# Eight-batch attention and mixer: the last 64 tokens of two batches in one chunk of 128 rows

## The chip, the cores and the metric

The kernel runs on one core of one Trainium2 chip. The metric is the device time of a launch in microseconds, median of three runs. Of one more execution there is a profile; its span goes from the first to the last instruction.

## The reference

For each of 8 batches with 8 heads, 576 tokens and head dimension 64, a linear attention ("cosformer") is followed by a mixer of tokens and channels:

```
phi(x) = [relu(x)*cos, relu(x)*sin]            # 128 features a head; cos, sin of the token's position
x   = phi(q) (phi(k)^T v) / (phi(q) sum_s phi(k) + 1e-6)     # [8, 576, 512] with heads side by side
u   = x + (relu(x^T w_tok1) w_tok2)^T          # w_tok1 [576, 256], w_tok2 [256, 576]
out = u + relu(u w_ch1) w_ch2                  # w_ch1 [512, 1536], w_ch2 [1536, 512]
```

## The kernel before

A batch's 576 tokens are four chunks of 128 rows (`ci` 0 to 3) and a tail of 64 tokens (`ci` = `R` = 4). Everything is kept for all 128 partitions, so the tail is folded: heads 0 to 3 (or channels 0 to 255) of its 64 tokens lie in partitions 0 to 63, heads 4 to 7 (channels 256 to 511) of the same tokens in partitions 64 to 127.

A batch goes through two parts:

- `Front(b)`: features of k and q (`feature`, VectorE, written as `k_side`, `q_side`), values (`values`, mostly ScalarE), `kv` (eight matmuls of 65 columns a chunk), transposed q features (`q_trans_dma` by DMA transposes, `q_trans` on TensorE for batches 0 and 1), `num` (eight matmuls of 65 columns a chunk, then reciprocal and product on VectorE into `x_sb`), token mixing `tok1` (sum over the chunks into two `b_ps`, relu into `B`) and `tok2` (`u_ps`, the sum `u_sb` on VectorE, the copy `u_bf` on ScalarE), and the transposes of u for the channel part by DMA (`u_trans_dma`: chunks 0 to 2 in one transfer, chunk 3 and the tail in a second).
- `Channel(b)`: twelve c steps (`c_main`: four matmuls of 512 columns into `c_ps`, relu by ScalarE into `h1T`; `c_tail`: four of 64 columns into `ct_ps`), then the o steps (`o_step`: twelve matmuls of 512 columns a chunk, two a step; for the tail twelve pairs of 256 columns, one of a pair writing partitions 0 to 63, the other 64 to 127), the sum `o_sb` on VectorE and the output DMA.

The order is written out by hand. While the steps of `Channel(b)` go through TensorE, the pieces of `Front(b + 1)` are put between them: `pieces` gives a slot number to each (C + n is behind c step n, O + n behind o step n), and each engine takes its instructions in that order. `first` is the plan for batch 1, which differs: its q is transposed on TensorE (slots C+9 to O+1), and batch 0's `tok2`, which has no transposes by DMA, lies in slots C+3 to C+7 of channel 0. Batch 0's own front (`first_front`) runs ahead of everything, and turns its u by matmuls (`turned_x`, `turned_b`). All loads, DMA transposes and nearly all stores are issued by SP, in program order.

Pools: PSUM has four one-bank buffers (`ps_mm`: `c_ps`, `ct_ps`, `o_ps`, `b_ps`, `u_ps`) and two of two banks (`ps_at`: `num_ps`, `kv_ps`, `qT_ps`, and `u_ps` of batch 0).

Of the kernel before, what the change touches and what calls it, by code (L numbers as in the profile page):

```python
# [16 lines left out]
def kernel(  # L17
# [15 lines left out]
    nc = tc.nc  # L33
# [31 lines left out]
    keep = ctx.enter_context(tc.tile_pool(name="keep", bufs=2))  # L65
    o_out = ctx.enter_context(tc.tile_pool(name="o_out", bufs=4))
    phi = ctx.enter_context(tc.tile_pool(name="phi", bufs=NSC))
# [20 lines left out]

    def load_tail(dst, src, b):
        return [nc.sync.dma_start(out=dst[half(g), 0:HH, R * D:(R + 1) * D],  # L90
                                  in_=src[b, g * HH:(g + 1) * HH, SM:S, :]
                                  .rearrange("h s d -> s h d"))
                for g in range(2)]

    def tiles():
        return tuple(io.tile([P, H, NSC * D], F32, name=n) for n in ("qt", "vt", "kt"))

    io_tiles = {0: tiles()}
    qt0, vt0, kt0 = io_tiles[0]
    load_main(qt0, q, 0, 0, HH)  # L100
    load_main(qt0, q, 0, HH, H, nc.scalar)
    load_tail(qt0, q, 0)
    load_main(kt0, k, 0, 0, HH)
    k_done = load_main(kt0, k, 0, HH, H)
    load_tail(kt0, k, 0)
    load_main(vt0, v, 0, 0, HH)
    load_tail(vt0, v, 0)
    load_main(vt0, v, 0, HH, H)

    stage = keep.tile([P, NSC, Dm], F32, name="u_sb").rearrange("p c m -> p (c m)")  # L110
    w_tok1n = stage[:, 0:R * D_tok].rearrange("p (r t) -> p r t", r=R)
    w_tok2n = stage[:, R * D_tok:R * D_tok + NT * S].rearrange("p (n s) -> p n s", n=NT)
# [10 lines left out]
    w_tail1 = const.tile([P, 2, D_tok], BF16, name="w_tail1")  # L123
    w_tok2 = const.tile([P, NT, S], BF16, name="w_tok2")
# [15 lines left out]
    sin_t = const.tile([P, NSC + 2], F32, name="sin_t")  # L140
    cos_t = const.tile([P, NSC + 2], F32, name="cos_t")
    for t, bias, sc in ((sin_t, bias0, scale), (cos_t, bias_hp, -scale)):
        nc.vector.memset(t, 0.0)
        nc.scalar.activation(t[:, 0:NSC], theta, AF.Sin, bias=bias, scale=sc)
        for g in range(2):
            nc.vector.tensor_copy(t[half(g), NSC + g:NSC + g + 1], t[half(g), R:NSC])

    ones = const.tile([P, 3], BF16, name="ones")
    nc.gpsimd.memset(ones, 1.0)
    for g in range(2):  # L150
        nc.gpsimd.memset(ones[half(1 - g), 1 + g:2 + g], 0.0)


    v_augs = []
    for i in range(2):
        va = const.tile([P, NSC, H, DP], BF16, name=f"v_aug{i}")
        nc.vector.memset(va[:, :, :, D:D1], 1.0)
        v_augs.append(va)


    for g in range(2):
        nc.vector.memset(w_tail1[half(1 - g), g, :], 0.0)
    for g in range(2):
        nc.gpsimd.dma_start(out=w_tail1[half(g), g, :], in_=moe_w_tok1[SM:S, :])
# [26 lines left out]
    def permute_tok2(ki):  # L191
        nc.scalar.copy(w_tok2[:, ki, 0:SM].rearrange("t (r p) -> t r p", r=R),
                       w_tok2n[:, ki, 0:SM].rearrange("t (p r) -> t r p", r=R))
        nc.scalar.copy(w_tok2[:, ki, SM:S], w_tok2n[:, ki, SM:S])


    class Front:
        def __init__(self, b, res):
            self.qt, self.vt, self.kt = io_tiles[b]
            self.va = v_augs[b % 2]  # L200
            self.res = res

            self.padded = b > 0
            self.kp, self.qp = {}, {}

            self.qpT = once.tile([P, NSC * H, P], BF16, name="qpT")
            self.kv_sb = [small.tile([P, HH, DP], BF16, name=f"kv_sb{g}") for g in range(2)]
            self.x = once.tile([P, NSC, Dm], BF16, name="x_sb")

        def feature(self, which, ci, j, heads=(0, H), on_act=False):  # L210
            dst, src = (self.kp, self.kt) if which == "k" else (self.qp, self.qt)
            if ci not in dst:
                dst[ci] = phi.tile([P, H, 2, D], BF16, name=which + "p")
            if ci < R:
                parts = [(*heads, heads[0], ci)]
            elif self.padded:
                parts = [(g * HH, (g + 1) * HH, 0, NSC + g) for g in range(2)]
            else:
                parts = [(0, HH, 0, R)]
            for lo, hi, at, col in parts:  # L220
                w = (cos_t, sin_t)[j][:, col:col + 1]
                o_ap = dst[ci][:, lo:hi, j, :]
                i_ap = src[:, at:at + hi - lo, ci * D:(ci + 1) * D]
                if on_act:
                    nc.scalar.activation(o_ap, i_ap, AF.Relu, bias=bias0, scale=w)
                else:
                    nc.vector.tensor_scalar(o_ap, i_ap, scalar1=w, scalar2=0.0,  # L227
                                            op0=ALU.mult, op1=ALU.max)

        def values(self, ci, eng, heads=(0, H)):  # L230
            lo, hi = heads if ci < R else (0, HH)
            src = self.vt[:, lo:hi, ci * D:(ci + 1) * D]
            dst = self.va[:, ci, lo:hi, 0:D]
# [5 lines left out]
        def ksum(self, ci, heads=(0, H)):  # L239

            if not hasattr(self, "ks_ps"):
                self.ks_ps = ps_mm.tile([P, H], F32, name="ks_ps", tag="mm")
                self.ks_first = True
            for h in range(*heads):
                i, col = (h, 0) if ci < R else (h % HH, 1 + h // HH)
                nc.tensor.matmul(self.ks_ps[:, h:h + 1],
                                 self.kp[ci][:, i, :, :].rearrange("p a b -> p (a b)"),
# [8 lines left out]
        def dens(self, ci):  # L256

            if ci == 0:
                self.d_ps = ps_mm.tile([P, R * H + HH], F32, name="d_ps", tag="mm")
                self.d_sb = small.tile([P, R * H + HH, 1], F32, name="d_sb")  # L260
            if ci < R:
                each = [(slice(0, P), ci * H + h, h) for h in range(H)]
            else:
                each = [(half(g), R * H + j, g * HH + j) for j in range(HH) for g in range(2)]
            for rows, i, h in each:
                nc.tensor.matmul(self.d_ps[rows, i:i + 1], self.qpT[:, i, rows],
# [6 lines left out]
        def kv(self, ci, halves=(0, 1)):  # L273
            if ci == 0 and not hasattr(self, "kv_ps"):
                self.kv_ps = {}
                if self.padded:
                    both = ps_at.tile([P, 2, 512], F32, name="kv_ps", tag="at")
                    self.kv_ps = {g: both[:, g, :] for g in range(2)}
            if ci == 0 and not self.padded:
                for g in halves:  # L280
                    self.kv_ps[g] = ps_at.tile([P, 2, 512], F32, name="kv_ps", tag="at")[:, 0, :]
            if ci < R or self.padded:
                each = [(g, j, slice(0, P), g * HH + j) for g in halves for j in range(HH)]
            else:
                each = [(g, j, half(g), j) for j in range(HH) for g in halves]
            for g, j, rows, i in each:
                nc.tensor.matmul(self.kv_ps[g][:, j * DP:j * DP + D1],  # L287
                                 self.kp[ci][rows, i, :, :].rearrange("p a b -> p (a b)"),
                                 self.va[rows, ci, i if ci < R else j, 0:D1],
                                 start=(ci == 0 and j == 0),  # L290
                                 stop=(ci == NSC - 1 and j == HH - 1),
                                 skip_group_check=True)
# [8 lines left out]
        def q_trans(self, ci, heads=(0, H), eng=nc.scalar):  # L301
            lo, hi = heads if ci < R or self.padded else (0, HH)
# [4 lines left out]
            for h in range(lo, hi):  # L307
                nc.tensor.transpose(qT_ps[:, h - lo, :],  # L308
                                    self.qp[ci][:, h, :, :].rearrange("p a b -> p (a b)"), ident)
            dst = self.qpT[:, ci * H + lo:ci * H + hi, :]  # L310
# [5 lines left out]
        def q_trans_dma(self, ci):  # L316
            nc.sync.dma_start_transpose(out=self.qpT[:, ci * H:(ci + 1) * H, :],
                                        in_=self.qp[ci].rearrange("p h a b -> p (h a b)"))

        def num(self, ci, fill=0, dens=False):  # L320
# [3 lines left out]
            n = 2 if ci < R else 1  # L324
            for h in range(H):
                g, j = divmod(h, HH) if ci < R else (h % 2, h // 2)
                kv = self.kv_sb[g][:, j, 0:D1]
                cols = slice(j * DP, j * DP + D1)
                if ci < R:
                    nc.tensor.matmul(num_ps[:, g, cols], self.qpT[:, ci * H + h, :], kv,  # L330
                                     start=True, stop=True)
                elif self.padded:
                    nc.tensor.matmul(num_ps[:, 0, cols], self.qpT[:, R * H + g * HH + j, :], kv,
                                     start=(g == 0), stop=(g == 1))
                else:
                    nc.tensor.matmul(num_ps[half(g), 0, cols], self.qpT[:, R * H + j, half(g)], kv,
                                     start=True, stop=True)
            nv = num_ps[:, 0:n, 0:HH * DP].rearrange("p g (j d) -> p g j d", d=DP)
            if dens:
                den = self.d_sb[:, ci * H:ci * H + n * HH, :].rearrange("p (g j) o -> p g j o", g=n)  # L340
            else:
                den = small.tile([P, 2, HH, 1], F32, name="den")[:, 0:n]
# [3 lines left out]
                self.x[:, ci, 0:n * DH].rearrange("p (g j d) -> p g j d", g=n, j=HH),  # L346
# [406 lines left out]
```

## Time and profile before

| what | value |
|---|---|
| runs | 274.5, 274.86, 273.28 us (median 274.5) |
| span of the profiled execution | 271.7 us |
| around the span, against the median | 2.8 us |
| TensorE (PE) busy | 262.8 us, 97% |
| VectorE (DVE) busy | 165.4 us, 61% |
| ScalarE (ACT) busy | 123.8 us, 46% |
| DMA moved | 54.46 MB, 200 GB/s |
| granted TensorE clock | 1.000 |

The profiled execution has no launch time of its own, so its time is taken as its span and the 2.8 us by which the median of the runs lies above it. Busy time of TensorE counts overlapping matmuls once, and its ends are modelled; what one matmul costs in a stream is therefore read from start to start, not from its own duration (a matmul of 512 columns lasts 379 ns, and the next starts 215 ns after it).

### The profile page before, as it was taken

How to read it: one execution, taken by the hardware profiler on the slowest of the kernel's cores; microseconds unless marked ns; L12 is line 12 of the kernel's file. 1: busy time of each engine (PE TensorE's matmuls, PEld its weight loads, DVE VectorE, ACT ScalarE, POOL GpSimd, SP SyncE). 2: the span in 40 equal slices, each digit the busy share in tenths (PEclk: the TensorE clock that was granted, in tenths of full speed). 3: DMA queues.
4: the chain of work that ended last, by engine and by line, in shares of the span. 5: the costliest groups of instructions: out<-in, count | busy, mean ns of one | idle time of the engine just before them, and what ended most of it. 6: DMA issues, size and time to landing. Idle time of an engine off the chain costs nothing.

```text
span 271.7 us, 5917 instructions
## 1 busy us (share of the span) xinstructions
PE 262.8 (97%) x2386; PEld 145.5 (54%) x2414; DVE 165.4 (61%) x421; ACT 123.8 (46%) x235; POOL 7.8 (3%) x21
## 2 busy tenths in 40 slices
PE   7989999999999999999999999999999999999994
PEld 2566466445555456455555455455555455454542
DVE  4954696759466495649666596639666586630031
ACT  4963882055616264236616264236625364315500
POOL 3400300000000000000000000000000000000000
PEclk9999999999999999999999999999999999999999
DMA  7999999959994889868696988769795453061022
GB/s 214 371 258 300 318 189 274 355 65 297 198 321 91 240 228 215 278 161 275 134 281 186 281 165 237 243 159 278 156 325 137 151 117 80 39 183 41 0 80 97
DMA packets 95483, 54.46 MB, mean 200 GB/s; under 512 B 62688, under 2 KB 90976, under 8 KB 95456
## 3 DMA queue, kind: packets, MB, share of 16 engines
q1 hardware_dynamic: 92016, 50.28, 66.7%
q0 software_dynamic: 2832, 3.21, 7.1%
q10 hardware_dynamic: 608, 0.59, 0.7%
q8 instruction: 19, 0.31, 0.5%
q14 instruction: 8, 0.07, 0.1%
HBM read 35.85 MB, written 9.44 MB: 167 GB/s over the span
## 4 chain that ended last, share of the span: by engine, by line
PE 92%; ACT 3%; DMA 2%; DVE 1%; issue 1%; POOL 0%; POOLq 0%; ACTq 0%
PE o_ps L535 29%; PE c_ps L501 29%; PE b_ps L358 5%; PE u_ps L386 4%; PE ct_ps L520 4%; PE kv_ps L287 4%; PE idle_ps L186 3%; PE o_ps L539 3%; PE num_ps L330 3%; DMA uT<-u_bf 2%; ACT qpT L312 1%; PE b_ps L362 1%; PE c_ps L511 1%; PE u_ps L390 1%; PE qT_ps L308 1%
## 5 line engine op out<-in xcount | busy, mean ns | idle before, releaser
L535 PE MATMUL o_ps<-w_ch,h1T 128*128 128x512 bf16 x367 | 94.1, 379 | 1.2
L501 PE MATMUL c_ps<-uT,w_ch 128*128 128x512 bf16 (+2 forms) x384 | 92.2, 372 | 1.0 <-DMA uT<-u_bf 0.9
L505 ACT ACTIVATE h1T<-c_ps 128x512 bf16<-128x512 f32 x93 | 55.7, 601 | 62.6 <-PE c_ps L501 62.4
L545 DVE TENSOR_TENSOR o_sb<-o_ps,u_sb 128x512 f32<-128x512 f32 (+1 forms) x40 | 25.4, 635 | 53.1 <-PE o_ps L535 49.6
L535 PEld LDWEIGHTS <-h1T 128*128 128x128 bf16 x384 | 35.1, 98 | 35.6 <-issue 1.6
L501 PEld LDWEIGHTS <-w_ch 128*128 128x128 bf16 x384 | 32.5, 97 | 29.2 <-DMA uT<-u_bf 1.4
L520 PEld LDWEIGHTS <-w_ch 128*128 128x128 bf16 x384 | 22.0, 98 | 18.4
L393 DVE TENSOR_TENSOR u_sb<-u_ps,x_sb 128x512 f32<-128x512 f32 (+1 forms) x40 | 24.7, 633 | 9.8 <-PE u_ps L386 9.5
L395 ACT CAST u_bf<-u_sb 128x512 bf16<-128x512 f32 (+1 forms) x35 | 19.4, 574 | 18.5 <-DVE u_sb L393 16.9
L520 PE MATMUL ct_ps<-uT,w_ch 128*128 128x64 bf16 x384 | 24.1, 193 | 0.0
L368 ACT ACTIVATE B<-b_ps 128x512 bf16<-128x512 f32 x8 | 4.8, 597 | 42.1 <-PE b_ps L358 42.1
L345 DVE TENSOR_TENSOR x_sb<-num_ps,den 128x512 bf16<-128x512 f32 (+1 forms) x35 | 22.3, 638 | 1.2
L227 DVE TENSOR_SCALAR qp<-qt,cos_t 128x512 bf16<-128x512 f32 (+1 forms) x50 | 20.4, 419 | 0.9 <-DMA qt<-in_q_dram 0.9
L227 DVE TENSOR_SCALAR qp<-qt,sin_t 128x512 bf16<-128x512 f32 (+1 forms) x50 | 20.4, 419 | 0.0
L227 DVE TENSOR_SCALAR kp<-kt,cos_t 128x512 bf16<-128x512 f32 (+1 forms) x47 | 20.0, 442 | 0.3 <-DMA kt<-in_k_dram 0.3
L235 ACT CAST v_aug<-vt 128x512 bf16<-128x512 f32 (+1 forms) x34 | 18.1, 556 | 0.0
L358 PE MATMUL b_ps<-x_sb,w_tok 128*128 128x512 bf16 x63 | 17.7, 379 | 0.1
L386 PE MATMUL u_ps<-B,w_tok 128*128 128x512 bf16 x57 | 17.6, 379 | 0.1
L227 DVE TENSOR_SCALAR kp<-kt,sin_t 128x512 bf16<-128x512 f32 (+1 forms) x42 | 17.5, 430 | 0.0
L343 DVE TENSOR_SCALAR den<-num_ps 128x8 f32<-128x8 f32 (+1 forms) x35 | 5.7, 164 | 18.3 <-PE num_ps L330 17.7
L287 PE MATMUL kv_ps<-v_aug,kp 128*128 128x65 bf16 (+1 forms) x320 | 15.5, 193 | 0.3 <-ACT qpT L312 0.3
L330 PE MATMUL num_ps<-kv_sb,qpT 128*128 128x65 bf16 x256 | 14.0, 193 | 0.7 <-DVE x_sb L345 0.5
(80 smaller groups left out, 186.3 us busy)
## 6 DMA issues: line engine op xcount, KB each, us to landing
out_dram<-o_sb SPq DMA_DIRECT2D x32, 256.0 KB, 3.7
kt<-in_k_dram SPq DMA_DIRECT2D x7, 1024.0 KB, 5.9
qt<-in_q_dram SPq DMA_DIRECT2D x7, 1024.0 KB, 7.9
vt<-in_v_dram SPq DMA_DIRECT2D x7, 1024.0 KB, 6.5
w_ch<-in_moe_w_ch_dram POOLq DMA_DIRECT2D x4, 384.0 KB, 9.8
w_ch<-in_moe_w_ch_dram POOLq DMA_DIRECT2D x3, 512.0 KB, 8.8
qt<-in_q_dram SPq DMA_DIRECT2D x16, 64.0 KB, 6.2
kt<-in_k_dram SPq DMA_DIRECT2D x2, 512.0 KB, 6.5
```

The lines of the kernel that those rows point to most:

```text
L227: nc.vector.tensor_scalar(o_ap, i_ap, scalar1=w, scalar2=0.0, op0=ALU.mult, op1=ALU.max)
L287: nc.tensor.matmul(self.kv_ps[g][:, j * DP:j * DP + D1], self.kp[ci][rows, i, :, :].rearrange("p a b -> p (a b)"), self.va[rows, ci, i if ...
L330: nc.tensor.matmul(num_ps[:, g, cols], self.qpT[:, ci * H + h, :], kv, start=True, stop=True)
L345: nc.vector.tensor_mul(self.x[:, ci, 0:n * DH].rearrange("p (g j d) -> p g j d", g=n, j=HH), nv[:, :, :, 0:D], den.to_broadcast([P, n, HH, ...
L358: nc.tensor.matmul(self.b1_ps[mi], w_tok1[:, ci, cols], self.x[:, ci, :], start=(ci == 0), stop=(ci == R - 1))
L386: nc.tensor.matmul(u_ps, w_tok2[:, ki, ci * P:(ci + 1) * P], self.B1[:, ki, :], start=(ki == 0), stop=(ki == NT - 1))
L393: nc.vector.tensor_add(res["u"][:, ci, 0:n], u_ps[:, 0:n], self.x[:, ci, 0:n])
L501: nc.tensor.matmul(c_ps[:, lo:hi], w_ch1[:, ki, mi * P:(mi + 1) * P], uT[:, lo // P:hi // P, ki, :], start=(ki == 0), stop=(ki == NCC - 1))
L505: nc.scalar.activation(self.h1T[:, mi, 0:SM], c_ps, AF.Relu)
L520: nc.tensor.matmul(self.ct_ps[:, mi % 6, :], w_ch1[:, ki, mi * P:(mi + 1) * P], self.res["uT"][:, R * NCC + ki % 2, half(ki // 2)], start= ...
L535: nc.tensor.matmul(o_ps, self.h1T[:, ki, ci * P:(ci + 1) * P], w_ch2[:, ki, :], start=start, stop=stop)
L545: nc.vector.tensor_add(o_sb[:, 0:n], o_ps[:, 0:n], res["u"][:, ci, 0:n])
```

## The change

The tails of two batches (2p and 2p + 1) are put together in one chunk of 128 rows: the even batch's 64 tokens in partitions 0 to 63, the odd batch's in 64 to 127, all eight heads (512 channels) in the free dimension. A class `Tail` holds what a pair shares.

- Features of k and q of the tail are made once a pair, in the even batch's front (two instructions of 128x512 for k, two for q, instead of four and four of 128x256 for each batch); batches 0 and 1 still make their own, on 64 partitions. The DMA transpose of the q features is issued once a pair. The loads of both batches' tails come with the even batch's loads.
- `values`, `num`'s product, `tok2`'s sum and copy of the tail work on the batch's own 64 partitions, with 512 elements instead of 256. The other half of `v_aug` and of the new `x_tail` is set to zero once, so that `kv` and `tok1` can use all 128 rows.
- `tok1` and `tok2` of the tail are one matmul of 512 columns where there were two of 256; `tok2` now makes 128 rows, of which a batch uses its 64.
- The transposes of u of the tail, and its c and o, are made once a pair, in the odd batch's channel part: `c_tail` is four matmuls of 128 columns for each of 12 blocks, `o_step(R)` twelve of 512 columns. Channels of even batches have 12 c and 24 o steps and no tail, channels of odd batches 12 and 30.
- Batch 0's tail is no longer turned by matmuls ahead of its channel; its u is copied by ScalarE (`ub_tail`) behind `tok2` in slot C+7.
- The plan of an odd batch's front (3, 5, 7) has `kv` of chunk 3 and of the tail, `kv_out`, `num`, the mixing and the transposes of u one slot earlier.
- In the last channel the tail's o comes first, and chunk 3 is made last, in two halves of 256 columns.

The core of the diff:

```diff
+    class Tail:
+
+        def __init__(self, pair):
+            self.qt, self.vt, self.kt = io_tails[pair]
+            self.kp = twos.tile([P, H, 2, D], BF16, name="kp_tail")
+            self.qp = once.tile([P, H, 2, D], BF16, name="qp_tail")
+            self.qpT = twos.tile([P, H, P], BF16, name="qpT_tail")
+
+        def new_u(self):
+            self.u = twos.tile([P, Dm], F32, name="u_tail")
+            self.ub = once.tile([P, Dm], BF16, name="ub_tail")
+            self.uT = once.tile([P, NCC, P], BF16, name="uT_tail")
...
+                t = self.tail
+                dst, src = (t.kp, t.kt) if which == "k" else (t.qp, t.qt)
+                rows = self.rows if self.alone else slice(0, P)
+                w, o_ap, i_ap = w[rows], dst[rows, lo:hi, j, :], src[rows, lo:hi, :]
...
-                if ci < R:
-                    nc.tensor.matmul(self.b1_ps[mi], w_tok1[:, ci, cols], self.x[:, ci, :],
-                                     start=(ci == 0), stop=(ci == R - 1))
-                else:
-                    for g in range(2):
-                        nc.tensor.matmul(self.b1_ps[mi][:, g * DH:(g + 1) * DH],
-                                         w_tail1[:, g, cols], self.x[:, R, 0:DH],
-                                         start=False, stop=False, skip_group_check=True)
+                w = w_tok1[:, ci, cols] if ci < R else w_tail1[:, cols]
+                nc.tensor.matmul(self.b1_ps[mi], w, self.x_of(ci),
+                                 start=(ci == ORDER[0]), stop=(ci == ORDER[-1]))
...
-                for g in range(2):
-                    nc.tensor.matmul(u_ps[half(g), 0:DH], w_tok2[:, ki, SM:S],
-                                     self.B1[:, ki, g * DH:(g + 1) * DH],
-                                     start=(ki == 0), stop=(ki == NT - 1))
...
+                nc.tensor.matmul(u_ps, w_tok2[:, ki, ci * P:(ci + 1) * P],
+                                 self.B1[:, ki, :], start=(ki == 0), stop=(ki == NT - 1))
+            u = res["u"][:, ci, :] if ci < R else tail.u[rows]
+            nc.vector.tensor_add(u, u_ps[rows], self.x_of(ci)[rows])
+            if ci == R:
+                nc.scalar.copy(tail.ub[rows], u)
+            elif turn:
+                nc.scalar.copy(self.ub[:, ci, :], u)
...
+        def tail_trans_dma(self):
+            nc.sync.dma_start_transpose(out=self.tail.uT, in_=self.tail.ub)
...
+                plan += [(C + at, KV, ci) for ci, at in
+                         enumerate((2, 3, 4, 5, 6) if odd else (2, 3, 4, 6, 7))]
+                plan.append((C + (7 if odd else 8), self.kv_out))
             if first:
                 at, mix, t = (O + 4, O + 6, O + 7, O + 9, O + 10), O + 11, O + 14
+            elif odd:
+                at, mix, t = (C + 8, C + 9, C + 10, C + 11, O + 2), O + 3, O + 7
             else:
                 at, mix, t = (C + 9, C + 10, C + 11, O + 1, O + 3), O + 4, O + 8
...
-            plan += [(t + 2, self.u_trans_dma, 0, 3), (t + 3, self.u_trans_dma, 3, NSC)]
+            plan += [(t + 2, self.u_trans_dma, 0, 3), (t + 3, self.u_trans_dma, 3, R)]
+            if odd:
+                plan.append((t + 3, self.tail_trans_dma))
...
-                nc.tensor.matmul(self.ct_ps[:, mi % 6, :], w_ch1[:, ki, mi * P:(mi + 1) * P],
-                                 self.res["uT"][:, R * NCC + ki % 2, half(ki // 2)],
+                nc.tensor.matmul(self.ct_ps[:, mi % R, :], w_ch1[:, ki, mi * P:(mi + 1) * P],
+                                 self.tail.uT[:, ki, :], start=(mi % R == 0 and ki == 0),
...
-                for g in range(2):
-                    nc.tensor.matmul(o_ps[half(g), 0:DH], self.h1T[:, ki, SM:S],
-                                     w_ch2[:, ki, g * DH:(g + 1) * DH], start=start, stop=stop)
...
+                h = self.h1T[:, ki, ci * P:(ci + 1) * P] if ci < R else self.h1T_tail[:, ki, :]
+                nc.tensor.matmul(o_ps, h, w_ch2[:, ki, cols], start=ki == 0, stop=ki == NCH - 1)
...
-                rest = (2, R, 3)
-            else:
-                rest = range(NSC) if self.b == B - 1 else (0, 1, R, 2, 3)
+                rest = (2, 3)
+            elif self.b == B - 1:
+                rest = (R, 0, 1, 2)
+            else:
+                rest = (0, 1, R, 2, 3) if self.b % 2 else range(R)
             for ci in rest:
                 o_range(ci, 0, NCH)
+            if self.b == B - 1:
+
+                for g in range(2):
+                    steps.append(lambda g=g: self.o_step(R - 1, 0, NCH,
+                                                         slice(g * DH, (g + 1) * DH)))
```

More of the change, by code (lines that the diff above doesn't have):

```diff
@@ L204, in __init__, with k_of @@
             self.kp, self.qp = {}, {}
-            self.qpT = once.tile([P, NSC * H, P], BF16, name="qpT")
-            self.kv_sb = [small.tile([P, HH, DP], BF16, name=f"kv_sb{g}") for g in range(2)]
-            self.x = once.tile([P, NSC, Dm], BF16, name="x_sb")
+            self.qpT = once.tile([P, R * H, P], BF16, name="qpT")
+            self.kv_sb = [twos.tile([P, HH, DP], BF16, name=f"kv_sb{g}") for g in range(2)]
+            self.x = once.tile([P, R, Dm], BF16, name="x_sb")
+        def k_of(self, ci):
+            return self.kp[ci] if ci < R else self.tail.kp
@@ L210, in feature, with q_of, qT_of, x_of @@
+        def q_of(self, ci):
+            return self.qp[ci] if ci < R else self.tail.qp
+        def qT_of(self, ci, h):
+            return self.qpT[:, ci * H + h, :] if ci < R else self.tail.qpT[:, h, :]
+        def x_of(self, ci):
+            return self.x[:, ci, :] if ci < R else self.xt
+        def rows_of(self, ci):
+            return slice(0, P) if ci < R else self.rows
         def feature(self, which, ci, j, heads=(0, H), on_act=False):
-            dst, src = (self.kp, self.kt) if which == "k" else (self.qp, self.qt)
@@ L275, in kv @@
                 self.kv_ps = {}
-                if self.padded:
+                if halves == (0, 1):
                     both = ps_at.tile([P, 2, 512], F32, name="kv_ps", tag="at")
                     self.kv_ps = {g: both[:, g, :] for g in range(2)}
-            if ci == 0 and not self.padded:
+            if ci == 0 and halves != (0, 1):
                 for g in halves:
                     self.kv_ps[g] = ps_at.tile([P, 2, 512], F32, name="kv_ps", tag="at")[:, 0, :]
[L282 to L292, printed above, removed]
+            for g in halves:
+                for j in range(HH):
+                    nc.tensor.matmul(self.kv_ps[g][:, j * DP:j * DP + D1],
+                                     self.k_of(ci)[:, g * HH + j, :, :]
+                                     .rearrange("p a b -> p (a b)"),
+                                     self.va[:, ci, g * HH + j, 0:D1],
+                                     start=(ci == 0 and j == 0),
+                                     stop=(ci == NSC - 1 and j == HH - 1),
+                                     skip_group_check=True)
         def kv_out(self, halves=(0, 1), eng=None):
@@ L372, in tok2 @@
         def tok2(self, ci, pool=None, turn=True):
-            res = self.res
+            res, tail = self.res, self.tail
             if ci == 0:
-                res["u"] = keep.tile([P, NSC, Dm], F32, name="u_sb")
+                res["u"] = keep.tile([P, R, Dm], F32, name="u_sb")
                 if turn:
                     self.new_uT()
-                    self.ub = once.tile([P, NSC, Dm], BF16, name="u_bf")
+                    self.ub = once.tile([P, R, Dm], BF16, name="u_bf")
+            if ci == R and not hasattr(tail, "u"):
+                tail.new_u()
             if pool is None:
@@ L382, in tok2 @@
                 u_ps = pool.tile([P, Dm], F32, name="u_ps", tag="at")
-            n = Dm if ci < R else DH
+            rows = self.rows_of(ci)
             for ki in range(NT):
-                if ci < R:
-                    nc.tensor.matmul(u_ps, w_tok2[:, ki, ci * P:(ci + 1) * P],
-                                     self.B1[:, ki, :], start=(ki == 0), stop=(ki == NT - 1))
-                    continue
-                for g in range(2):
-                    nc.tensor.matmul(u_ps[half(g), 0:DH], w_tok2[:, ki, SM:S],
-                                     self.B1[:, ki, g * DH:(g + 1) * DH],
-                                     start=(ki == 0), stop=(ki == NT - 1))
@@ new lines, in tok2, with turned_x @@
+            u = res["u"][:, ci, :] if ci < R else tail.u[rows]
[4 more added lines that the diff above has]
+                nc.scalar.copy(self.ub[:, ci, :], u)
+        def new_uT(self):
+            self.res["uT"] = keep.tile([P, R * NCC, P], BF16, name="uT")
+        def turned_x(self, dst, kb, first):
+            for ci in range(R):
+                nc.tensor.matmul(dst[:, ci * P:(ci + 1) * P],
+                                 self.x[:, ci, kb * P:(kb + 1) * P], ident, start=first,
+                                 stop=False, skip_group_check=True)
@@ L549, in o_step @@
                 return
             for g in range(2):
-                eng = nc.scalar if b == B - 1 and g == 1 else nc.sync
-                eng.dma_start(out=out[b, SM:S, g * DH:(g + 1) * DH], in_=o_sb[half(g), 0:DH])
+                nc.sync.dma_start(out=out[b - 1 + g, SM:S, cols], in_=o_sb[half(g)])
         def steps(self, done):
```

288 lines of the change are left out of this document (132 added, 156 removed).

## The prediction

> **What bounds the kernel.** First the page's busy shares and the chain that ended last:
>
> ```profile
> PE 262.8 (97%) x2386; PEld 145.5 (54%) x2414; DVE 165.4 (61%) x421; ACT 123.8 (46%) x235; POOL 7.8 (3%) x21
> ...
> PE 92%; ACT 3%; DMA 2%; DVE 1%; issue 1%; POOL 0%; POOLq 0%; ACTq 0%
> ```
>
> TensorE is the bound; nearly all else waits for it. So the change is worth what it takes from TensorE's stream, less what others then make TensorE wait. The chain in order of time tells what a matmul costs in the stream:
>
> ```profile
> 57.07 4.69 DMA uT<-u_bf
> 61.81 2.79 PE c_ps L501 x24
> ...
> 92.50 2.59 PE c_ps L501 x12
> ...
> 116.28 1.31 PE o_ps L539 x24
> ...
> 122.88 2.59 PE c_ps L501 x12
> ...
> 247.10 0.86 PE c_ps L501 x4
> 248.09 0.86 PE c_ps L501 x4
> ```
>
> A channel lasts 122.88 - 92.50 = 30.38 us, all of it streaming. 512 columns cost 2.59/12 = 0.2155 us. At 61.81, 12 matmuls have 384 columns and 12 have 128; start to start in the trace these cost 0.1625 and 0.0557, each with weights of its own (2.62; the rest of 2.79 is the last one's drain). A tail's c in channel 7 takes 248.09 - 247.10 - 0.86 = 0.12 for four, 0.0293 each start to start. A pair of tail-o matmuls takes 1.31/12 = 0.109: its halves run side by side. So cost goes by columns, and folding the tail already made its columns few. TensorE's timeline shows what surrounds such half matmuls:
>
> ```profile
> 115.35 0.59 PE L386 MATMUL u_ps<-B,w_tok 128*128 128x512 bf16 x2
> 115.87 0.41 PE L390 MATMUL u_ps<-B,w_tok 128*64 128x256 bf16 x4
> 116.11 1.48 PE L539 MATMUL o_ps<-w_ch,h1T 128*64 128x256 bf16 x24
> 117.52 0.82 PE L535 MATMUL o_ps<-w_ch,h1T 128*128 128x512 bf16 x3
> ```
>
> The two matmuls at 115.35 are through at 115.78; the next full one starts at 117.52. The stretch, 1.74, is 14 pairs (1.53) and two changes of width, 0.1 each.
>
> **Steady channels.** c of the tail: 96 x 0.0293 = 2.81 a pair of batches before, 48 x 0.0557 = 2.67 after. `tok2` and o of the tail: 2 x 1.74 = 3.48 before; 2 x 0.431 + 12 x 0.2155 = 3.45 after. `kv`, `num` and `tok1` keep their columns. So the pair saves only 0.17: an even channel loses 1.41 + 1.74 - 0.43 = 2.72, an odd one gains 1.26 + 1.28 = 2.54.
>
> Waits. `num(0)` follows `kv_out` by one c step. Before: relu starts 0.2 behind c, takes 0.5, the two kv copies end 0.68 later (timeline at 102.2 to 103.4), so `num` ends 1.52 behind that c, 0.18 late. In an even channel the c step now lacks 0.24 of tail: 0.41 late. In an odd one tail columns double: not late. Per pair +0.05. The q transposes: VectorE drops the tail features (1.05 for k, 1.05 for q ahead of the last), so q of chunk 0 lands 7.3 us into the channel (96.45 + 3.16 - 92.33) as now, against 9.0 needed; chunk 3 about 12, against 14. Covered by over 1.5 us. The transposes of u in an even channel: second one issued 3.1 behind `tok2(2)`, landing 5.65 (2.55 as at 118.66), with 6.9 until the next channel; covered by 1.25. The tail's own transposes are queued behind on SP, ahead of stores and the next k load, which have a channel's time. On ScalarE and VectorE the tail's `values`, product, sums and copies go from 256 to 512 elements (0.42 to 0.69 us on VectorE), while half the features go: hidden at 61% and 46% busy; uncovered they would cost 0.27 each. Batches 2 to 5: 2 x (-0.17 + 0.05) = -0.24. Batches 6 and 7: -2.72 + 0.23 + 1.26 + (2.59 - 1.41) = -0.05.
>
> **Head.** Batch 0's tail is no longer turned: 12 matmuls of 64 columns, -0.35. Its wider features, copies and products, on 64 partitions, are priced by the 128x512 rows (no row is on 64 partitions; between the 256 and the 512 price, I take the upper): +0.1 where k's arrival and the wait for x3 do not cover them. The zero fills fall ahead of q's landing at 5.8.
>
> **Channel 0 decides.** It gives its tail c (1.41) and tail o (1.4) to channel 1, which gets 2.54 more. Does channel 0 become shorter by that?
>
> ```profile
> 36.25 0.41 DVE L393 TENSOR_TENSOR u_sb<-u_ps,x_sb 128x256 f32<-128x256 f32 x1
> 37.33 1.01 ACT L312 COPY qpT<-qT_ps 128x1024 bf16<-128x1024 bf16 x1
> 40.52 1.95 ACT L312 COPY qpT<-qT_ps 128x1024 bf16<-128x1024 bf16 x2
> 42.52 0.89 PE L287 MATMUL kv_ps<-v_aug,kp 128*128 128x65 bf16 x24 [0.31 <-ACT qpT L312]
> ```
>
> `kv` at 42.52 waits for ScalarE's last copy, and ScalarE is full from 36.8 on. The new `ub_tail` copy (C+7) stands in ScalarE's queue ahead of h1T(8) and all four copies, and waits for the tail's sum on VectorE, which has the k features and q(0) in front of it. VectorE's rows, moved by the head and with the two 0.4 us tail features, end that sum at 35.94; then copy 0.53, four relus of 0.5, four copies of 0.92: 42.15. `kv` comes 0.3 earlier, where TensorE alone would come 2.3 earlier (bounds 0 and -2.3; the ScalarE order is the nearer row). Then the tail's product takes 0.69 instead of 0.42, and `b_ps` L362 at 50.17 had only 0.06 to spare behind it: 0.3 is lost again. `tok2(2)` ends at 55.5 as before.
>
> From there TensorE needed 5.2 to the channel's end, and waited until 6.3 for the transposes at 57.07 (the 4.69 above). After, it needs 0.43 x 3 + 6 x 0.431 = 3.88. Issued at +1.57, the transposes land at +4.8 if they take 3.23 as in channel 2 (116.48 to 119.71), at +6.3 if 4.69. The DMA view of 57 to 62 us, in slices of 0.125, shows why they took longer:
>
> ```profile
> DMA  0000000000769999000000000019999999989999
> ...
> q8 instruction: 1, 0.02, 1.7%
> ```
>
> They stop from 59.0 to 60.3, after a 16 KB instruction packet began at 58.32. The page has 19 of these for 4830 TensorE instructions, one in 254. By the order of the instructions that place now falls some 70 ahead of `tok2(2)`, so I take 3.23: channel 1 starts 1.45 earlier. Its first tail c needs the tail's u transposed: issued third on SP at +5.1, landing +7.65, needed at +7.45: +0.2.
>
> **End.** Before, tail last, 3.75 from the last matmul to the end. After, half of chunk 3, 128 KB in one store: between 2.19 (64 KB) and 2.48 (256 KB) to landing, +0.15, and +0.03 for halves. For an instruction packet among the transposes of channel 6, +0.15.
>
> **The sum**, against the profiled execution (span 271.7 + 2.8 = 274.5, the median): -1.45 to the start of channel 1, + 2.54 - 0.18 + 0.2 in it, -0.24 - 0.05 for the other pairs, +0.18 and +0.15 at the end: +1.1, or 275.6. A measurement of this kernel can tell about 0.5%, 1.4 us, from no change.
>
> **Rivals.**
> 1. *The transposes wait in channel 0 stays* (4.69, or `kv` no earlier). The idle that the moved tail leaves is then wholly filled by the wait at 61.81: +2.6, 277.1. For: it is there now. Against: the interrupting packet moves. 0.28.
> 2. *Even channels end in a wait.* Cover of 1.25 is less than one interruption (1.4), and loads with two tails each are larger; at 0.9 in each of three channels, 278.3. It decides once the second transposes take over 3.8; they now take 2.55. 0.12.
> 3. *Faster.* ScalarE's order does not bind and the wait at 61.81 goes: `kv` 2.3 earlier and no loss at L362 put the start of channel 1 3.75 earlier: -3.75 + 2.56 - 0.29 + 0.33 = -1.15; without the 0.95 of waiting for the transposes that is left, -2.1, 272.4. For: ScalarE had 1.2 us idle between 34 and 36.8. Against: nearly all waits must vanish. 0.08.
> 4. *Weights not hidden.* A 98 ns weight load (page, L520's rows) showing behind each 0.0557 matmul would cost 192 x 0.042 = 8, 282.6. Against it stand the 12 at 61.81. 0.02.
> 5. That the change leaves the work where it was: TensorE's order after has 4102 instructions for 4830, so no.
>
> A rule that speaks against the change bears on rival 4: by the Trainium skill, page "TensorE: Matmul & The Clock Gate", section "Back-to-back issue gap", pairs of weight load and matmul are spaced about 81 ns at 128 columns. By that the tail's c would take 5 us more than I count, an estimate. The trace disagrees: 0.0557.
>
> **Chances.** My sum 0.50, its own range 274.4 to 276.9: within 0.5% 0.37, slower 0.12, faster 0.01. With rivals 1 and 2 slower, 3 mostly faster, 4 slower: faster 0.07, same 0.41, slower 0.52. The likeliest single case is the sum. 273.8 to 278.0 leaves out rival 4, most of 3, half of 2.
>
> **What would show it.** Right: `ct_ps` and tail `o_ps` together within 0.3 us a pair of the old; ScalarE idle behind the tail's sum near C+7, `kv` of batch 1 at about 42; even channels near 27.9 us, odd near 32.7; channel 1's c at about 60.4. Wrong: matmuls of 128 columns spaced by over 60 ns; waits for `uT` ahead of channels 3, 5, 7; `kv` of batch 1 near 40.

## The result, and the profile after

The changed kernel takes 275.64 us (median of 6, 275.25 to 276.44) where the kernel before, run beside it, takes 274.15 (273.28 to 274.86): a ratio of 1.0065, 95% interval [1.0046, 1.0084]. A second series gave 275.35 to 273.76, 1.0059 [1.0037, 1.0080]. So the change costs 1.5 to 1.6 us. Medians below are of up to 12 executions; where some of these had a granted clock of 0.991 to 0.994, these mostly lie 1.5 to 3.7 us above the others, which widens the intervals.

The profiled execution took 275.3 us. Its page gives the span, then for each engine the busy time, its share of the span and the number of instructions, then the shares of the chain that ended last.

```profile
span 273.5 us, 5131 instructions
PE 263.8 (96%) x2050; PEld 139.3 (51%) x2050; DVE 163.8 (60%) x374; ACT 128.8 (47%) x232; POOL 9.6 (4%) x22
PE 85%; DVE 6%; ACT 3%; DMA 3%; issue 1%; POOL 0%; POOLq 0%; ACTq 0%
```

There are 336 matmuls fewer (2050 for 2386), and TensorE is busy for 1.0 us more: the work was regrouped, not removed. TensorE's part of the chain fell from 92% to 85%: more of the end now hangs on VectorE, ScalarE and DMA. Where, the chain in order of time shows (start, length, what). First channel 0:

```profile
35.16 0.60 DVE u_tail L412
35.78 0.62 ACT ub_tail L414
36.40 0.97 ACT h1T L528 x2
...
40.15 1.81 ACT qpT L347 x2
42.01 0.89 PE kv_ps L321 x24
...
56.98 3.31 DMA uT<-u_bf
60.34 2.79 PE c_ps L524 x24
```

The new copy `ub_tail` waits for the tail's sum on VectorE, and everything from there to `kv` at 42.01 is ScalarE. The transposes of u now take 3.31 instead of 4.69. TensorE's timeline shows two more places (start, length, instructions; in brackets the idle time before and what ended it):

```profile
104.02 0.42 PE L362 MATMUL num_ps<-kv_sb,qpT 128*128 128x65 bf16 x8 [0.22 <-DMA qpT<-qp]
268.14 1.47 PE L557 MATMUL o_ps<-w_ch,h1T 128*128 128x256 bf16 x12 [0.52 <-DVE o_sb L562]
```

In channel 2 a q transpose landed late; the chain has it as

```profile
99.03 4.94 DMA qpT<-qp
```

At 268.14 the second half of the last chunk waits until VectorE has read the first half, since both halves lie in one PSUM tile.

The starts of the channels (first `c_ps` matmul in the timeline) and their lengths; the last column reaches to the start of the last matmul:

| | ch. 1 starts | ch. 1 | ch. 2 | ch. 3 | ch. 4 | ch. 5 | ch. 6 | ch. 7 |
|---|---|---|---|---|---|---|---|---|
| before | 61.81 | 30.52 | 30.38 | 30.38 | 30.38 | 30.38 | 30.38 | 23.44 |
| after | 60.34 | 32.79 | 28.31 | 32.75 | 27.91 | 32.75 | 27.91 | 26.59 |
| difference | -1.47 | +2.27 | -2.07 | +2.37 | -2.47 | +2.37 | -2.47 | +3.15 |

Channels 1 to 6 together change by 0.00. What channel 0 gains (1.47) is less than what channel 7 loses (3.15); with +0.14 behind the last matmul (3.89 for 3.75) that is +1.8 in the span.

### The profile page after: what moved, and what is told of

The parts are those of the page before. It is cut to its first block, busy times and chain, and to the rows that moved or that the text cites. A ratio compares the mean times of both kernels' runs of the same rounds, so it can differ in the third digit from the quotient of the medians.

```text
span 273.5 us, 5131 instructions
## 1 busy us (share of the span) xinstructions
PE 263.8 (96%) x2050; PEld 139.3 (51%) x2050; DVE 163.8 (60%) x374; ACT 128.8 (47%) x232; POOL 9.6 (4%) x22
## 4 chain that ended last, share of the span: by engine, by line
PE 85%; DVE 6%; ACT 3%; DMA 3%; issue 1%; POOL 0%; POOLq 0%; ACTq 0%
PE o_ps L557 31%; PE c_ps L524 24%; PE b_ps L385 6%; PE u_ps L409 6%; PE ct_ps L544 4%; PE idle_ps L205 4%; PE num_ps L362 3%; PE kv_ps L321 3%; DMA qpT<-qp 2%; DVE kp L264 1%; ACT qpT L347 1%; DMA uT<-u_bf 1%; ACT h1T L528 1%; DVE x_sb L372 1%; PE c_ps L534 1%
## 5 line engine op out<-in xcount | busy, mean ns | idle before, releaser
L557 PE MATMUL o_ps<-w_ch,h1T 128*128 128x512 bf16 (+1 forms) x396 | 95.1, 372 | 0.5 <-DVE o_sb L562 0.5
L524 PEld LDWEIGHTS <-w_ch 128*128 128x128 bf16 x384 | 33.1, 97 | 30.1 <-DMA uT<-u_bf 1.4
L412 DVE TENSOR_TENSOR u_sb<-u_ps,x_sb 128x512 f32<-128x512 f32 x32 | 22.1, 689 | 9.7 <-PE u_ps L409 9.6
L416 ACT CAST u_bf<-u_sb 128x512 bf16<-128x512 f32 x28 | 17.3, 618 | 17.6 <-DVE u_sb L412 17.6
L409 PE MATMUL u_ps<-B,w_tok 128*128 128x512 bf16 x80 | 22.8, 379 | 0.1
L372 DVE TENSOR_TENSOR x_sb<-num_ps,den 128x512 bf16<-128x512 f32 x28 | 19.4, 691 | 1.0
L544 PEld LDWEIGHTS <-w_ch 128*128 128x128 bf16 x192 | 14.0, 98 | 9.2
L385 PE MATMUL b_ps<-x_sb,w_tok 128*128 128x512 bf16 x64 | 17.9, 379 | 0.0
L544 PE MATMUL ct_ps<-uT_tail,w_ch 128*128 128x128 bf16 x192 | 17.2, 219 | 0.0
L264 DVE TENSOR_SCALAR qp<-qt,sin_t 128x512 bf16<-128x512 f32 (+1 forms) x35 | 15.8, 451 | 0.0
L362 PEld LDWEIGHTS <-qpT 128*128 128x128 bf16 x256 | 11.6, 98 | 7.6 <-issue 2.1
L264 DVE TENSOR_SCALAR kp<-kt,cos_t 128x512 bf16<-128x512 f32 x32 | 15.2, 479 | 0.4 <-DMA kt<-in_k_dram 0.4
```

Of the source, the lines that this page charges most:

```text
L362: nc.tensor.matmul(num_ps[:, g, j * DP:j * DP + D1], self.qT_of(ci, h), self.kv_sb[g][:, j, 0:D1], start=True, stop=True)
L372: nc.vector.tensor_mul(self.x_of(ci)[rows].rearrange("p (g j d) -> p g j d", g=2, j=HH), nv[:, :, :, 0:D], den.to_broadcast([rows.stop - r ...
L385: nc.tensor.matmul(self.b1_ps[mi], w, self.x_of(ci), start=(ci == ORDER[0]), stop=(ci == ORDER[-1]))
L409: nc.tensor.matmul(u_ps, w_tok2[:, ki, ci * P:(ci + 1) * P], self.B1[:, ki, :], start=(ki == 0), stop=(ki == NT - 1))
L412: nc.vector.tensor_add(u, u_ps[rows], self.x_of(ci)[rows])
L416: nc.scalar.copy(self.ub[:, ci, :], u)
```

## Experiments

The theory: TensorE's cost goes by columns, so sharing tails moves work and saves 0.1 to 0.2 us a pair; the loss is waits, in channel 0 (the emptied time is not used), in even channels (`num(0)` behind `kv_out`), and at the end (one PSUM tile). Rivals: narrow matmuls dearer than their columns; the features or the transposes of q bind.

**The changed kernel again**, beside the second group of variants.

> The changed kernel itself once more, on the same chip as the variants beside it, for their comparison. Expected 1.0 to 2.2 us over the kernel before.

275.35 to 273.76, +1.59; channel 1 starts at 59.88, the rest is as above except channel 2 (28.11). So channel 0's end and channel 2 differ between executions by some 0.5, the other channels by 0.01.

**The tail's c and o left out, after and before.** In both kernels `c_tail` is not called and `o_step(R)` puts out u:

```diff
-                    for m in range(tails[0], upto):
-                        self.c_tail(m)
...
+            if ci == R:
+                if hi == NCH:
+                    nc.vector.tensor_copy(o_sb, self.tail.u)
+                    ...
+                return
```

> The changed kernel with the tail's c and o matmuls left out (the tail's output is u alone; its front part stays). Theory (48 c matmuls at 0.0557 and 12 o matmuls at 0.2155 are 5.26 us a pair, and nothing hides): odd channels 27.5 to 27.7, even ones 27.9 as they are, the launch about 21.0 us shorter, 254.4. Rival (128-column matmuls show their weight loads): 26 us or more shorter.

> The kernel before with the tail's c and o matmuls left out in the same way. Theory (1.41 for c and 1.31 to 1.4 for o a batch): channels 1 to 6 of 27.6 to 27.9 instead of 30.38, the last one 2.7 shorter, channel 0 shorter by 0 to 2.8; the launch 19 to 22 us shorter, 252 to 255, so that both kernels without tails lie within 2 us of each other, the difference being channel 0's. Rival (folded tails cost more than their columns, so that pairing saves several us on TensorE): 25 us or more shorter.

After: 257.92, 17.4 less than the 275.35 with tails. Before: 256.10, 17.5 less than the 273.59 beside it. Both missed the expected saving (21.0; 19 to 22), because waits came up where the tails had been. In the first, channel 2 now stops for 1.82:

```profile
99.91 0.42 PE L362 MATMUL num_ps<-kv_sb,qpT 128*128 128x65 bf16 x8 [1.82 <-DMA qpT<-qp]
```

This transpose of q was issued at 93.07 and landed at 99.86, 1.5 behind the last store issued ahead of it (98.36). The odd channels of the first last 28.5 to 28.6, not 27.5: two of three end in a wait for the transposes of u (0.57 and 0.45), and in all three, as in channels 2 to 6 of the second, `num(0)` comes late behind `kv_out`, as in the changed kernel's even channels (0.41, see the run with `kv_out` earlier). Channel 3 of the second:

```profile
127.78 0.56 PE L330 MATMUL num_ps<-kv_sb,qpT 128*128 128x65 bf16 x8
128.18 1.03 PE L501 MATMUL c_ps<-uT,w_ch 128*128 128x512 bf16 x4
129.04 0.41 PE L330 MATMUL num_ps<-kv_sb,qpT 128*128 128x65 bf16 x8
129.28 1.03 PE L501 MATMUL c_ps<-uT,w_ch 128*128 128x512 bf16 x4
```

The late one takes 0.40 until the next c, the one after it 0.24.

So that the two kernels without tails lie 1.8 apart, about as far as with them, says little: other waits make up this distance. Channel 7, which has no front beside it, gives the clean figure: in the first it is 26.59 - 21.31 = 5.28 shorter, and 48 matmuls of 0.0557 and 12 of 0.2155 make 5.26. So the rival of dear narrow matmuls falls. Its row says the same:

```profile
74.62 0.67 PE ct_ps L544 x12
```

Two channels together last 2 x 30.38 = 60.76 before and 32.75 + 27.91 = 60.66 after: a pair saves 0.10, its waits included.

**The copy `ub_tail` later.** Batch 0's copy goes from C+7 behind o step 3:

```diff
-            if ci == R:
+            if ci == R and turn:
                 nc.scalar.copy(tail.ub[rows], u)
...
+            slots.setdefault(NCH + 3, []).append((f.tail_copy, ()))
```

> The changed kernel, with batch 0's copy of the tail's sum on ScalarE (ub_tail, slot C+7 of channel 0) moved behind o step 3. Theory (ScalarE's order holds kv in channel 0: the copy waits 2.14 us for VectorE's sum and the four qpT copies stand behind it): kv at about 40.5 instead of 42.0, channel 1 starts at about 58.9 instead of 60.3, the launch 1.5 us shorter. Rival (the transposes of q or VectorE bind, the copy's place is irrelevant): kv at 41.7 or later and no more than 0.3 us in the time.

274.80 (12), 1.0044 [1.0015, 1.0074] against before. Its chain:

```profile
33.23 1.41 DVE kp_tail L264 x2
...
35.60 0.64 PE qT_ps L343 x8
36.26 1.01 ACT qpT L347
...
41.05 0.89 PE kv_ps L321 x24
```

ScalarE takes up `qpT` at 36.26 instead of 37.38, and `kv` comes at 41.05 instead of 42.01 (41.48 in the second profile of the changed kernel): 0.4 to 1.0 earlier, not 1.5. Channel 1 starts at 59.41. The copy's place does count, so the rival's 0.3 is passed, but only two thirds or less of the expected is there: the next to bind is the tail's k features on VectorE at 33.23, which the q features and so the first `qT_ps` wait for. These two took 0.68 and 0.81 there, beside DMA issues of GpSimd, and 0.48 each in the second profile of the changed kernel; without these 0.53, `kv` would come at 40.5, as expected (an estimate). But the profile that the 42.0 comes from had lost 0.41 in the same way. In the time the gain can't be told from none.

**The first plan one slot earlier as well.**

```diff
-                at, mix, t = (O + 4, O + 6, O + 7, O + 9, O + 10), O + 11, O + 14
+                at, mix, t = (O + 3, O + 5, O + 6, O + 8, O + 9), O + 10, O + 13
```

> The changed kernel with batch 0's copy of the tail's sum behind o step 3 (as in the run that moved this copy alone: channel 1 at 59.41, with 0.90 us of waiting for the first transposes of u) and the first plan's num, mixing, tok2 and transposes of u one slot earlier. Theory (the wait ahead of channel 1 is the transposes' latency less the o work behind tok2, so one o step of 0.43 more behind it shortens the wait by that): channel 1 at about 59.0, the wait 0.5, the launch 0.4 us shorter than with the copy alone and about 1.7 shorter than the changed kernel. Rival (num then waits for kv_out, and b_ps for x_tail, for as long): channel 1 at 59.3 or later.

275.13, 1.0062 [1.0035, 1.0089]. The profile has channel 1 at 59.08, as expected, but the wait shrank by 0.05 (0.85 for 0.90), not by 0.43: against the run before, the transposes were issued 0.71 earlier and took 3.71 instead of 3.34. No gain in the time.

**Two PSUM tiles for the last chunk's halves.**

```diff
-            if lo == 0 and cols.start == 0:
+            if lo == 0:
```

> The changed kernel, with the two halves of the last chunk's o in the last channel in PSUM tiles of their own. Theory (the second half waits 0.52 us because the sum on VectorE still reads the tile that it writes): the gap at 268.1 goes, the launch 0.5 to 0.65 us shorter. Rival (the wait is only for VectorE as the engine that hands out buffers, or the store at the end takes its place): 0 to 0.2 us.

274.63, 1.0017 [0.9992, 1.0041]. The gap is gone; o runs without a stop:

```profile
264.79 4.73 PE L557 MATMUL o_ps<-w_ch,h1T 128*128 128x512 bf16 x33
```

Channel 7 lasts 25.91 instead of 26.59: 0.68. The theory holds.

**`kv_out` one slot earlier in odd batches' fronts.**

```diff
-                         enumerate((2, 3, 4, 5, 6) if odd else (2, 3, 4, 6, 7))]
-                plan.append((C + (7 if odd else 8), self.kv_out))
+                         enumerate((2, 3, 4, 5, 5) if odd else (2, 3, 4, 6, 7))]
+                plan.append((C + (6 if odd else 8), self.kv_out))
```

> The changed kernel; in the plan of odd batches' fronts kv of the tail is put into the slot of chunk 3's (C+5) and kv_out one slot earlier (C+6), so that two c steps lie ahead of num(0). Theory (num(0) in even channels waits about 0.4 us for the copies of kv): three even channels 0.3 to 0.4 us shorter each, the launch 0.7 to 1.2 us shorter. Rival (kv now waits for the features or values instead, or num's wait is for the transposed q): -0.2 to +0.6 us.

274.51, 1.0006 [0.9981, 1.0031]. Channels 4 and 6 last 27.50 instead of 27.91, 0.41 less each, the upper end of what was expected; channel 2, whose q transpose came late again (4.70), 28.10. In the changed kernel `num(0)` starts 0.26 behind the eight c matmuls ahead of it (8 x 0.2155) and takes 0.39 until the next c; with the edit it follows twelve without a gap and takes 0.25:

```profile
161.44 1.89 PE L524 MATMUL c_ps<-uT,w_ch 128*128 128x512 bf16 x8
163.43 0.56 PE L362 MATMUL num_ps<-kv_sb,qpT 128*128 128x65 bf16 x8
163.82 1.03 PE L524 MATMUL c_ps<-uT,w_ch 128*128 128x512 bf16 x4
```

```profile
162.26 2.76 PE L524 MATMUL c_ps<-uT,w_ch 128*128 128x512 bf16 x12
164.85 0.41 PE L362 MATMUL num_ps<-kv_sb,qpT 128*128 128x65 bf16 x8
165.10 1.03 PE L524 MATMUL c_ps<-uT,w_ch 128*128 128x512 bf16 x4
```

The theory holds.

**Features for each batch again.** `self.alone = True`, the odd fronts' KS, QS and q transposes of the tail back in the plan, and the unused half of the tail's features filled with zeros by GpSimd. Then the same with that fill behind batch 2's q load.

> The changed kernel, with the tail's features of k and q and their transpose made for each batch again instead of once a pair (on the batch's own 64 partitions; 12 more feature products of about 0.4 us on VectorE and three more transposes). Theory (the features lie beside TensorE's stream, so that saving them paid nothing): the time of the changed kernel within 0.3 us, the odd fronts' num without a new wait. Rival (VectorE's order holds the odd fronts, their saving is what lets kv and num lie one slot earlier): num(0) or num(1) waits in channels 2, 4 and 6, 0.3 us or more each, +0.9 us or more.

> The changed kernel with the tail's features and q transposes made for each batch again, as in the run before it (channels 2 to 7 as long as in the changed kernel, but channel 1 at 61.7), with the zero fill that this needs on GpSimd put behind batch 2's q load, so that it no longer lies at 34.7 to 35.9. Theory (what was lost there was VectorE's k_tail and q products, 1.50 and 1.16 instead of 0.48 us each, beside GpSimd's fill and DMA issues; the features themselves cost nothing): channel 1 at 59.9 to 60.4, the time within 0.4 us of the changed kernel. Rival (the extra features or transposes cost 0.8 us by themselves): channel 1 or the later channels later, 0.6 to 0.9 us over the changed kernel.

The first: 276.12, 1.0080 [1.0059, 1.0102], 0.8 above the changed kernel, against the theory. But it isn't the rival's place either: channels 4 and 6 last 27.91 as ever, channel 2 lasts 28.34, and it is channel 1 that starts late, at 61.71. Its timeline:

```profile
33.47 1.50 DVE L264 TENSOR_SCALAR kp_tail<-ktt,sin_t 64x512 bf16<-64x512 f32 x1
34.98 1.16 DVE L264 TENSOR_SCALAR qp<-qt,cos_t 128x512 bf16<-128x512 f32 x1
36.07 0.47 DVE L264 TENSOR_SCALAR qp<-qt,sin_t 128x512 bf16<-128x512 f32 x1
32.48 2.24 POOL L194 DMA_DIRECT2D w_ch<-in_moe_w_ch_dram  x3 [18.52 <-DMA qt<-in_q_dram]
34.69 1.17 POOL L722 MEMSET kp_tail<- 64x1024 bf16 x1
```

Two VectorE products took three and two and a half times their usual 0.47 beside GpSimd's issues and fill. With the fill moved away, the timeline has

```profile
33.52 0.47 DVE L264 TENSOR_SCALAR kp_tail<-ktt,sin_t 64x512 bf16<-64x512 f32 x1
34.00 0.52 DVE L264 TENSOR_SCALAR qp<-qt,cos_t 128x512 bf16<-128x512 f32 x1
```

channel 1 at 60.55, and 275.34, the changed kernel's time (ratio to before 1.0070 [1.0039, 1.0101]). So the saved features pay nothing that can be told, and the first variant's loss went with the fill. How much of the 1.50 was due to GpSimd's issues, which lie beside most of that product in this profile, stays open.

**The repairs together**: all four, and the three without the earlier first plan.

> The changed kernel with all four repairs: the copy of batch 0's tail sum later, the first plan one slot earlier, kv_out in odd fronts one slot earlier, two PSUM tiles for the last chunk's halves. Theory (the four waits are of different places and add up: 1.3 and 0.4 in channel 0, three times 0.41, 0.65 at the end): 3.4 to 3.8 us shorter than the changed kernel, about 1.5 to 2 us (0.6 to 0.7%) shorter than the kernel before; even channels 27.5, last channel 25.9. Rival (a wait that goes is replaced by the next one): less than 2 us shorter than the changed kernel.

> The changed kernel with three of the repairs: the copy of batch 0's tail sum later, kv_out in odd fronts one slot earlier, two PSUM tiles for the last chunk's halves; the first plan as it was. Theory (moving the first plan earlier brought nothing, since its transposes then met the tail loads of batch 2; the other three add up, 1.0, 0.7 to 1.2 and 0.65): 2.4 to 2.9 us shorter than the changed kernel, 0.2 to 0.5% faster than the kernel before. Rival (the earlier first plan was worth its 0.4): 273.5 or more, no faster than the kernel before.

All four: 273.33, 0.9982 [0.9956, 1.0009]; three: 273.54, 1.0005 [0.9979, 1.0032]. These are 2.0 and 1.8 less than the changed kernel, where 3.4 to 3.8 and 2.4 to 2.9 were expected; neither can be told from the kernel before. Even channels of 27.50 and the last of 25.91 are there; what is missing is channel 0 (59.64 and 60.75) and channel 2 (28.03, 28.14). In the profile of the three, channel 1 is 1.64 longer as well, at a lower clock of TensorE (last section). What holds channel 0 is seen when the variants stand side by side (us; times of landing as the trace has them for each transfer):

| | k of batch 1 landed | `kv` | transposes of u issued | last store ahead landed | transposes landed |
|---|---|---|---|---|---|
| after | 28.30 | 42.01 | 56.98 | 58.01 | 60.29 |
| after, again | 28.56 | 41.48 | 56.44 | 58.32 | 59.83 |
| two tiles | 28.34 | 42.42 | 57.39 | 59.40 | 60.89 |
| `kv_out` earlier | 29.86 | 43.15 | 58.12 | 60.68 | 62.19 |
| features each | 28.80 | 43.39 | 58.36 | 58.38 | 61.66 |
| the same, late fill | 28.62 | 41.77 | 56.74 | 59.00 | 60.51 |
| copy later | 28.23 | 41.05 | 56.03 | 57.87 | 59.36 |
| and first plan earlier | 28.07 | 40.76 | 55.32 | 57.46 | 59.03 |
| all four | 27.86 | 40.69 | 55.24 | 58.01 | 59.59 |
| three | 28.52 | 40.87 | 55.84 | 59.19 | 60.70 |

In each row the transposes land at the later of two times, within 0.1: 3.3 behind their issue, or 1.5 behind the landing of the last store of `o_sb` issued ahead of them. Issued more than 1.8 ahead of that landing, they gain nothing unless the store lands earlier, and it was issued behind batch 2's loads, which now carry the tails of two batches (two DMAs of 128 KB to a load, where there were two of 64 KB): the last of them landed at 54.80 and this store at 56.10 before, 56.72 and 58.01 after. That fits all ten rows, and the changed kernel without tails (issued at 57.15, landed at 60.45). In the kernel before and in the run that follows, where the store landed 1.0 and 1.2 ahead of the issue and an instruction packet fell among the transposes, it doesn't apply. No run moved those loads, so the cause is argued, not shown.

**The kernel before, moved in the instruction stream.**

```diff
-        busy(idle_ps, 12)
+        busy(idle_ps, 9)
+        busy(idle_ps[:, 0:16], 24)
```

> The kernel before, with its idle warm-up at the start made of 9 matmuls of 512 columns and 24 of 16 columns instead of 12 of 512, so that every later TensorE instruction moves by 21 matmuls in the stream and the work stays the same. Theory (a 16 KB instruction packet on a DMA queue holds up the transposes of u in channel 0, and its place goes by the count of instructions): the packet falls elsewhere, the transposes take about 3.2 instead of 4.69 us, the wait ahead of channel 1 (0.94) is gone, and channel 1 starts about 0.95 earlier; other channels may lose some of it where the packet now falls among their transposes. Rival (the first transposes are slow by themselves or by the loads around them): they still take 4.4 to 4.8 us and the time stays within 0.3 us.

272.74, 0.9954 [0.9929, 0.9978]: 1.2 us gained by changing no work. Channel 1 starts at 60.75, with this timeline and chain:

```profile
60.75 0.99 PE L501 MATMUL c_ps<-uT,w_ch 128*128 128x384 bf16 x5 [0.20 <-DMA uT<-u_bf]
```

```profile
56.75 3.96 DMA uT<-u_bf
```

The wait fell from 0.94 to 0.20, as the transposes took 0.73 less. The other 0.32 of the 1.06 by which channel 1 starts earlier lies ahead of them (`kv` at 42.19 for 42.52), and its cause is open. The packet did not leave the transposes' time: the trace has it at 57.59, 0.84 behind their issue (58.32 and 1.25 before), where it costs 0.7 instead of 1.4, against the 3.3 of the changed kernel's transposes. So the place of the packet counts, but the expectation that it would miss the transposes, and take the whole wait with it, was wrong.

## Why the prediction was right, and where it was wrong

The forecast of 275.6 against 275.64, slower with a chance of 0.52, was right. The parts:

- **Columns.** Right. `ct_ps` takes 0.67 for 12 matmuls (0.0557 each), a pair saves 0.10 (0.17 less 0.05 predicted), and this row, with the 5.28 of channel 7, excludes rival 4. (Its time would have been 283.6, with its 8 on top of the sum; nothing rests on that.)
- **`num(0)`** late by 0.41 in even channels, not in odd ones: right, and taking it away gives 0.41.
- **Channel 0.** Right: `kv` at 42.01 (42.15 predicted), transposes of 3.31 (3.23), channel 1 at 60.34 (60.4). Its reason, ScalarE's order, holds in part: with the copy moved, 0.4 to 1.0 comes back.
- **Tail transposes in channel 1**, +0.2: too much. Channel 1 is 0.04 longer than channels 3 and 5.
- **Covered by over 1.5 us** (the q transposes) failed in channel 2: 0.40 in the first profile, 0.20 in the second. An 8 KB and a 16 KB instruction packet (at 99.67 and 100.31) fell among them, and one took 4.94, where others take 2.79. By these rows it is rival 2's mechanism at another transfer, which the prediction had weighed only for the transposes of u; no run moved these packets, and with the copy moved both fell there too (4.48) and channel 2 lost nothing.
- **Batches 6 and 7**, -0.05: measured -2.47 + 3.15 = +0.68. The term that failed is "+0.03 for halves": making chunk 3 in two halves was priced as matmuls, and the wait of the second half for VectorE's read of the tile both share was overlooked. The run with two tiles gives 0.68.
- **End**: +0.15 predicted, +0.14.
- **Sum.** The span grew by 1.8, not by 1.1: +0.7 in channels 6 and 7 and +0.4 in channel 2 beyond the forecast, -0.3 in channel 1, and -0.2 since the packet expected among channel 6's transposes (0.15) cost nothing there (27.91, as channel 4) and the halves are counted above. That the number came out all the same is partly luck: the 2.8 us put around the span was 1.0 too much. The executions listed with their spans have 1.8 around it (275.3 and 273.5), so the profiled execution of before was one of about 273.5 and not of the median.

## What to carry to other kernels

Folding two half-empty tiles into a full one saves next to nothing where an instruction already costs what its columns cost; compare column counts before and after, not instruction counts. When work is moved off a stage, find what that stage waits for next (here a copy in ScalarE's queue, then VectorE's features, then, it seems, a transpose behind a store), and expect only the distance to it. Work split into halves needs two output buffers, or the second half waits for the first one's reader.

## What the runs showed of the hardware

- **VectorE beside GpSimd.** A product of 0.47 us took up to 1.50 while GpSimd issued DMAs or filled zeros. In the ten profiles of the changed kernel and its variants without that fill beside them, the products beside GpSimd's issues at 32 to 36 lost 0.04 to 0.76 in all. By the Trainium skill, page "SBUF — State Buffer", section "SBUF: two separate sides", the two engines share a port pair as an exclusive lock, and while GpSimd holds it a VectorE operation in a mode with two ports blocks. The longer products agree with that; in which mode they ran, no trace here shows.
- **Clock.** In the run with three repairs TensorE stood still for 2.43 us ahead of channel 1, and then had a mean granted clock of 0.65 for 4.3 us (third number from the end of the second row below, from the table by stage); from 62.0 to 65.4 it was 0.50:

```profile
60.75 4.13 PE L527 MATMUL c_ps<-uT,w_ch 128*128 128x384 bf16 x24 [2.43 <-DMA uT<-u_bf]
```

```profile
60.70:65.00 4.30, 4.25 (x28) 3.02 (x29) 4.30 (x12) 0.88 (x2) 0.00 (x0) 0.65 0.84 178
```

  The 24 matmuls took 4.13 instead of 2.79, and the channel lasted 34.43 instead of 32.79. After gaps of 1.63 (`kv_out` earlier, channel 1) and 1.82 (after without tails, channel 2) the clock stayed at 1. The Trainium skill, page "TensorE: Matmul & The Clock Gate", section "Why this matters for your kernels", warns of gaps over about 3 us; this one was 2.43. That the gap was the cause is likely, not shown: in the kernel before without tails the clock was 0.50 from 17.9 to 21.3, and the longest gap in the 8 us ahead of that was 0.28.
